# A fused token mixer and MLP on one core: a fixed order of all work, decay tables by exp, the state's sum off TensorE, w2 loaded in thirds, one-tile groups

## The chip, the cores and the metric

One core of a Trainium2 chip. The metric is device time in microseconds (us), median of several executions; lower is better. The kernel before takes 175.2 us. TensorE (PE in the profile) does matmuls and transposes, PEld loads its weights; VectorE is DVE, ScalarE is ACT, GpSimd is POOL, SyncE is SP, which issues most loads.

## The reference

A linear-attention recurrence per head, then a layer norm, an MLP and a residual. Float32 in and out, 4 batches, 8 heads of 48, 768 tokens, model width 384, MLP width 1536:

```python
for t in range(S):
    cur = np.einsum('bhd,bhe->bhde', u[None] * kt, vt)
    y[:, :, t] = np.einsum('bhd,bhde->bhe', rt, state + cur)
    state = w[None, :, :, None] * state + np.einsum('bhd,bhe->bhde', kt, vt)
...
xn = (x - mu) / np.sqrt(var + 1e-06) * g_ln
ch = np.maximum(xn @ w_ch1, 0.0) @ w_ch2
return x + ch
```

Both kernels cut the tokens into 24 tiles of 128. Within a tile the recurrence becomes matrix products: K is scaled by w to a falling power of the token's place, R by w to a rising one, both are transposed, their product is masked to the past, and the rest goes through a running state Z (bf16).

## The kernel before

It is tuned already: the tiles run in a rotation in which the MLP of earlier tiles fills TensorE while attention of the next tile waits for other engines. Four places matter here. The decay tables are made by doubling along the token axis on VectorE, transposed in float32 on TensorE and evicted:

```python
T = const.tile([P, 2 * CK, L + 1], FP32, name="T")
... # T[..., n+1:2n+1] = T[..., 1:n+1] * T[..., n], seven times, on VectorE
for a in (0, 1):
    for kc in range(CK):
        nc.tensor.transpose(out=fps[:, a, kc * P : (kc + 1) * P], in_=src, identity=ident_f[:])
```

The old state is added in PSUM by a matmul with the identity, and VectorE multiplies the sum by the decay of a tile:

```python
nc.tensor.matmul(out=s_ps[:, : HP * E2], lhsT=ident[:], rhs=Z_t[i - 1]..., start=False, ...)
... # + K^T V of this tile
nc.vector.tensor_tensor(out=Z[:], in0=s_ps..., in1=WLZ[:], op=ALU.mult)
```

The MLP works on pairs of tiles (GT = 2), so an up-projection matmul has 256 columns:

```python
hp = ps_h.tile([P, 2, GW], FP32, name="hp")      # GW = 256
for f in range(2):
    for kc in range(CK):
        nc.tensor.matmul(out=hp[:, f, :], lhsT=w1_sb[:, n, kc, fb*P:(fb+1)*P], rhs=xT_t[g][:, kc, :], ...)
nc.scalar.activation(out=hT_t[g][:, 2*m : 2*m+2, :], in_=hp[:], func=ACT.Relu)
```

w1 is loaded in thirds by SyncE between the tiles' loads, scaled by the norm's gain and cast to bf16 by three engines. w2 comes in one load, issued by GpSimd in the second turn of the main loop:

```python
if s == W2_SLOT:                                  # s == 1
    nc.gpsimd.dma_start(out=w2_sb[:], in_=w2_src)
```

Of the kernel before, what the change touches and what calls it, by code (L numbers as in the profile page):

```python
# [8 lines left out]
FP32 = mybir.dt.float32  # L9
# [3 lines left out]
ENG = mybir.EngineType  # L13


@with_exitstack
def kernel(
# [24 lines left out]
    GT = 2  # L42
    GW = GT * P
    E2 = 2 * D
    assert D <= DP and H % 2 == 0 and S % L == 0 and C % P == 0 and F % P == 0
    assert tuple(out.shape) == (B, S, C)

    const = ctx.enter_context(tc.tile_pool(name="const", bufs=1))
    ld = ctx.enter_context(tc.tile_pool(name="ld", bufs=7))
    sb2 = ctx.enter_context(tc.tile_pool(name="sb2", bufs=2))  # L50
    sb3 = ctx.enter_context(tc.tile_pool(name="sb3", bufs=3))
    sm = ctx.enter_context(tc.tile_pool(name="sm", bufs=4))
    xp = ctx.enter_context(tc.tile_pool(name="xp", bufs=14))
    ps_h = ctx.enter_context(tc.tile_pool(name="ps_h", bufs=2, space=bass.MemoryType.PSUM))
    ps = ctx.enter_context(tc.tile_pool(name="ps", bufs=1, space=bass.MemoryType.PSUM))

    ctx.enter_context(
        tc.manual_schedule(
            engines={ENG.PE, ENG.DVE, ENG.Activation, ENG.Pool, ENG.SP}
        )  # L60
    )


    rk_t, vf_t, v_t = {}, {}, {}

    def load(i, k_eng=None):
        b, c = divmod(i, NCH)
        s0 = c * L
        rk = ld.tile([P, 2, H, D], FP32, name="rk")
        vf = ld.tile([P, H, D], FP32, name="vf")  # L70
        (k_eng or nc.sync).dma_start(out=rk[:, 1], in_=k[b, :, s0 : s0 + L, :].rearrange("h t d -> t h d"))
        nc.sync.dma_start(out=rk[:, 0], in_=r[b, :, s0 : s0 + L, :].rearrange("h t d -> t h d"))
        nc.sync.dma_start(out=vf[:], in_=v[b, :, s0 : s0 + L, :].rearrange("h t d -> t h d"))
        rk_t[i], vf_t[i] = rk, vf

    w_c = const.tile([P, CK], FP32, name="w_c")
    nc.sync.dma_start(out=w_c[:], in_=bass.AP(tensor=w.tensor, offset=w.offset, ap=[[1, P], [P, CK]]))
    load(0, nc.scalar)
    w_p = const.tile([P, HP], FP32, name="w_p")
    u_p = const.tile([P, HP], FP32, name="u_p")  # L80
    nc.vector.memset(w_p[:], 0.0)
    nc.vector.memset(u_p[:], 0.0)
    for src, dst in ((w, w_p), (u, u_p)):
        for par in range(2):
            nc.scalar.dma_start(
                out=dst[par * DP : par * DP + D, :],
                in_=bass.AP(tensor=src.tensor, offset=src.offset + par * D, ap=[[1, D], [E2, HP]]),
            )
    g_sb = const.tile([P, CK], FP32, name="g_sb")
    nc.scalar.dma_start(out=g_sb[:], in_=moe_g_ln.rearrange("(kc p) -> p kc", p=P))  # L90
    load(1)
    NW = 3
    FW = F // NW
    w1_f = const.tile([P, NW, CK, FW], FP32, name="w1_f")
    w1_src = moe_w_ch1.rearrange("(kc p) (n f) -> p n kc f", p=P, n=NW)
    for n in range(NW):
        nc.sync.dma_start(out=w1_f[:, n], in_=w1_src[:, n])
    w1_sb = const.tile([P, NW, CK, FW], BF16, name="w1_sb")
    w2_sb = const.tile([P, FK, C], BF16, name="w2_sb")
    w2_src = moe_w_ch2.rearrange("(fk p) c -> p fk c", p=P)  # L100
    load(2)
    load(3)


    ident_f = const.tile([P, P], FP32, name="ident_f")
    make_identity(nc, ident_f[:])
    mask = const.tile([P, P], BF16, name="mask")
    nc.gpsimd.memset(mask[:], 0.0)
    nc.gpsimd.affine_select(
        out=mask[:],  # L110
        in_=mask[:],
        compare_op=ALU.is_ge,
        fill=1.0,
        base=0,
        pattern=[[-1, P]],
        channel_multiplier=1,
    )
    ident = const.tile([P, P], BF16, name="ident")
    nc.vector.tensor_copy(ident[:], ident_f[:])
    expo = const.tile([P, GT], FP32, name="expo")  # L120
    nc.vector.memset(expo[:], -0.5)
    NSC = 3
    sc_bufs = []
    for i in range(NSC):
        t_ = const.tile([P, 2, H, DP], BF16, name=f"sc{i}")
        nc.vector.memset(t_[:, :, :, D:DP], 0.0)
        sc_bufs.append(t_)
    WLZ = const.tile([P, HP, E2], FP32, name="WLZ")
    nc.vector.memset(WLZ[:], 0.0)
    uwI = const.tile([P, HP, 2], BF16, name="uwI")  # L130
    nc.vector.memset(uwI[:], 0.0)


    T = const.tile([P, 2 * CK, L + 1], FP32, name="T")
    nc.vector.memset(T[:, :, 0:1], 1.0)
    nc.vector.tensor_copy(T[:, 0:CK, 1], w_c[:])
    nc.vector.reciprocal(out=T[:, CK : 2 * CK, 1], in_=w_c[:])
    n = 1
    while n < L:
        nc.vector.tensor_tensor(  # L140
            out=T[:, :, n + 1 : 2 * n + 1],
            in0=T[:, :, 1 : n + 1],
            in1=T[:, :, n : n + 1].to_broadcast([P, 2 * CK, n]),
            op=ALU.mult,
        )
        n *= 2
    fps = ps.tile([P, 2, 512], FP32, name="at")
    F2 = const.tile([P, 2, H, D], FP32, name="F2")
    for a in (0, 1):
        for kc in range(CK):  # L150
            src = T[:, CK + kc, 1 : L + 1] if a else T[:, kc, 0:L]
            nc.tensor.transpose(out=fps[:, a, kc * P : (kc + 1) * P], in_=src, identity=ident_f[:])
    nc.scalar.copy(out=F2[:, 0], in_=fps[:, 0, :C].rearrange("p (h d) -> p h d", h=H))
    nc.vector.tensor_copy(out=F2[:, 1], in_=fps[:, 1, :C].rearrange("p (h d) -> p h d", h=H))


    wl = const.tile([P, HP], FP32, name="wl")
    nc.gpsimd.tensor_tensor(out=wl[:], in0=w_p[:], in1=w_p[:], op=ALU.mult)
    n = 2
    while n < L:  # L160
        nc.gpsimd.tensor_tensor(out=wl[:], in0=wl[:], in1=wl[:], op=ALU.mult)
        n *= 2
    assert n == L
    for par in range(2):
        p0 = par * DP
        nc.gpsimd.tensor_tensor(
            out=uwI[p0 : p0 + D, :, par], in0=u_p[p0 : p0 + D, :], in1=w_p[p0 : p0 + D, :], op=ALU.mult
        )
    for par in range(2):
        p0 = par * DP  # L170
        nc.gpsimd.tensor_copy(
            out=WLZ[p0 : p0 + D, :, par * D : (par + 1) * D],
            in_=wl[p0 : p0 + D, :].unsqueeze(2).to_broadcast([D, HP, D]),
        )


    g_neg = const.tile([P, CK], FP32, name="g_neg")

    def scale_w1(n):
        if n == 0:  # L180
            nc.vector.tensor_scalar(
                out=g_neg[:], in0=g_sb[:], scalar1=-1.0, scalar2=None, op0=ALU.mult
            )
        nc.scalar.activation(
            out=w1_sb[:, n, 0], in_=w1_f[:, n, 0], func=ACT.Copy, scale=g_neg[:, 0:1]
        )
        nc.vector.tensor_scalar(
            out=w1_sb[:, n, 1], in0=w1_f[:, n, 1], scalar1=g_neg[:, 1:2], scalar2=None, op0=ALU.mult
        )
        nc.gpsimd.tensor_scalar(  # L190
            out=w1_sb[:, n, 2],
            in0=w1_f[:, n, 2],
            scalar1=g_neg[:, 2:3],
            scalar2=1.0,
            op0=ALU.mult,
            op1=ALU.mult,
        )


    tr_t, cc_t, Z_t, A_t, x_t, mv_t, xn_t, q_t, st = {}, {}, {}, {}, {}, {}, {}, {}, {}  # L200

    def scale(i):
        sc = sc_bufs[i % NSC]
        nc.vector.tensor_tensor(out=sc[:, 1, :, :D], in0=rk_t[i][:, 1], in1=F2[:, 1], op=ALU.mult)  # L204
        nc.gpsimd.tensor_tensor(out=sc[:, 0, :, :D], in0=rk_t[i][:, 0], in1=F2[:, 0], op=ALU.mult)  # L205
        vv = ld.tile([P, H, D], BF16, name="vv")
        nc.gpsimd.tensor_copy(out=vv[:], in_=vf_t[i][:])  # L207
        v_t[i] = vv

    def transposes(i):  # L210
        sc = sc_bufs[i % NSC].rearrange("p a (q e) d -> p (a q) (e d)", e=2)
        tp = ps.tile([P, 2 * HP, P], BF16, name="tr")
        for j in range(2 * HP):
            nc.tensor.transpose(out=tp[:, j, :], in_=sc[:, j, :], identity=ident[:])  # L214
        tr = sb3.tile([P, 2, HP, P], BF16, name="trs")
        nc.scalar.copy(out=tr[:], in_=tp[:].rearrange("p (a q) t -> p a q t", a=2))  # L216
        q = sb2.tile([P, HP, P], BF16, name="q")
        nc.vector.tensor_tensor(out=q[:], in0=tr[:, 0], in1=tr[:, 1], op=ALU.mult)  # L218
        tr_t[i] = tr
        q_t[i] = q  # L220

    def scores(i):
        b, c = divmod(i, NCH)
        tr, q = tr_t[i], q_t[i]
        at = ps.tile([P, 2, HP, P], FP32, name="at")
        for p in range(HP):
            for par in range(2):
                p0 = par * DP
                nc.tensor.matmul(  # L229
                    out=at[:, par, p, :],  # L230
                    lhsT=tr[p0 : p0 + D, 1, p, :],
                    rhs=tr[p0 : p0 + D, 0, p, :],
                    start=True,
                    stop=True,
                )
# [272 lines left out]
```

## Time and profile before

| | before |
|---|---|
| median of 3 | 175.21 us (175.11 to 175.75) |
| span of the profiled execution | 173.4 us |
| TensorE saturated from | 31.0 us |
| last matmul ends | 169.9 us |
| TensorE busy | 85% of the span |

The body by itself, from the end of the ramp to the last matmul (view: busy time by stretch; columns: stretch, its length, busy us of PE, PEld, DVE, ACT, POOL with instruction counts, granted clock, DMA share, GB/s):

```profile
31.00:169.90 138.90, 134.65 (x1523) 101.02 (x1520) 94.72 (x189) 84.39 (x157) 56.09 (x81) 1.00 0.55 115
```

Of 138.9 us TensorE is busy in 134.65; no other engine is busy in more than 95. So a change that only speeds another engine gains nothing here. There are three places to win: the 31 us before it, TensorE's own work, and its last per cents of idle.

### The profile page before, as it was taken

Reading aid. Unit: us, or ns where it says so; the run is one execution under the profiler, and the core shown is the slowest. Engines: PE = TensorE matmul, PEld = TensorE weight load, DVE = VectorE, ACT = ScalarE, POOL = GpSimd, SP = SyncE. Lnnn points to the kernel's source line nnn. Section 1 sums busy time; section 2 is a strip of 40 time slices with the busy share of each in tenths; the row PEclk is TensorE's granted clock in tenths of the full one; section 3 lists DMA queues with packets and bytes.
Section 4 is the critical chain, followed back from the end, with each engine's and each line's share of the span. In section 5 each row is a group of like instructions: output and inputs, shape, how many; then the busy total and the mean of one; then the engine's idle time right before and its main releaser. Section 6 shows DMA issues by size and latency. Waiting matters only on the chain.

```text
span 173.4 us, 4126 instructions
## 1 busy us (share of the span) xinstructions
PE 146.9 (85%) x1646; PEld 110.4 (64%) x1646; DVE 113.9 (66%) x236; ACT 94.6 (55%) x173; POOL 74.7 (43%) x119
## 2 busy tenths in 40 slices
PE   0327453998999999999999999999999999999981
PEld 0215242695786877777768767777778687686640
DVE  4407959549788688678767976786768667840111
ACT  0313273385585774675666647656666577565410
POOL 2292699057426553374255335642752453120000
PEclk9999999999999999999999999999999999999999
DMA  5999999999954755874686568546954011101121
GB/s 98 163 351 316 186 181 177 200 190 150 199 114 95 169 114 104 167 155 89 140 165 147 110 110 183 131 105 135 181 112 119 0 49 45 33 18 45 45 93 46
DMA packets 82739, 22.69 MB, mean 131 GB/s; under 512 B 76960, under 2 KB 81568, under 8 KB 82720
## 3 DMA queue, kind: packets, MB, share of 16 engines
q1 hardware_dynamic: 78896, 21.04, 59.1%
q0 software_dynamic: 1552, 1.18, 4.6%
q10 hardware_dynamic: 2272, 0.20, 1.1%
q8 instruction: 13, 0.21, 0.6%
q14 instruction: 6, 0.05, 0.1%
HBM read 18.88 MB, written 4.72 MB: 136 GB/s over the span
## 4 chain that ended last, share of the span: by engine, by line
PE 76%; DVE 10%; ACT 8%; issue 2%; DMA 1%; POOL 1%; DVEq 0%; ACTq 0%
PE hp L374 27%; PE o L396 25%; PE tr L214 7%; PE at L229 4%; ACT xT L359 3%; ACT trs L216 3%; PE tr L358 3%; PE s L240 2%; PE s L260 2%; PE y L312 2%; DMA w_c<-in_w_dram 1%; PE s L251 1%; PE y L300 1%; DVE ot L405 1%; DVE stats L326 1%
## 5 line engine op out<-in xcount | busy, mean ns | idle before, releaser
L374 PE MATMUL hp<-xT,w_sb 128*128 128x256 bf16 x432 | 58.0, 276 | 2.7 <-ACT xT L359 2.7
L396 PE MATMUL o<-w_sb,hT 128*128 128x384 bf16 x288 | 56.3, 326 | 0.9 <-DVE ot L405 0.8
L381 ACT ACTIVATE hT<-hp 128x512 bf16<-128x512 f32 x72 | 42.9, 598 | 22.6 <-PE hp L374 22.1
L279 POOL TENSOR_TENSOR Vb<-vf,cc 128x384 f32<-128x384 f32 x24 | 20.2, 841 | 66.2 <-ACT cc L277 66.2
L374 PEld LDWEIGHTS <-w_sb 128*128 128x128 bf16 x432 | 40.3, 99 | 9.0 <-issue 3.8
L396 PEld LDWEIGHTS <-hT 128*128 128x128 bf16 x288 | 27.6, 98 | 13.6 <-issue 1.4
L270 DVE TENSOR_TENSOR A<-at,mask 128x512 bf16<-128x512 f32 x48 | 30.7, 682 | 1.3 <-PE at L229 1.3
L216 ACT COPY trs<-tr 128x1024 bf16<-128x1024 bf16 x24 | 24.2, 1009 | 13.2 <-PE tr L214 13.2
L218 DVE TENSOR_TENSOR q<-trs 128x512 bf16<-128x512 bf16 x24 | 12.3, 512 | 25.2 <-ACT trs L216 25.1
L205 POOL TENSOR_TENSOR sc<-rk,F 128x384 bf16<-128x384 f32 x24 | 23.9, 997 | 2.4 <-DMA rk<-in_r_dram 2.4
L405 DVE SCALAR_TENSOR_TENSOR ot<-o,rs,x 128x384 f32<-128x384 f32 x24 | 14.6, 609 | 14.6 <-PE o L396 14.6
L214 PE MATMUL tr<-ident,sc 128*128 128x128 bf16 x192 | 16.7, 234 | 7.4 <-POOL sc L205 5.7
L214 PEld LDWEIGHTS <-sc 128*128 128x128 bf16 x192 | 13.6, 105 | 10.2 <-POOL sc L205 6.5
L322 DVE TENSOR_TENSOR x<-y,Vb 128x384 f32<-128x384 f32 x24 | 13.4, 556 | 9.1 <-PE y L312 9.0
L337 ACT ACTIVATE xn<-x,mv 128x384 bf16<-128x384 f32 x24 | 14.8, 617 | 0.7 <-DVE mv L330 0.7
L277 ACT COPY cc<-s 128x8 f32<-128x8 f32 x24 | 4.0, 166 | 20.2 <-PE s L260 17.8
L359 ACT COPY xT<-tr 128x384 bf16<-128x384 bf16 x24 | 11.5, 480 | 5.5 <-PE tr L358 5.5
L204 DVE TENSOR_TENSOR sc<-rk,F 128x384 bf16<-128x384 f32 x24 | 14.4, 599 | 0.0
L207 POOL CAST vv<-vf 128x384 bf16<-128x384 f32 x24 | 14.3, 595 | 0.0
L326 DVE BATCH_NORM_STATS2 stats<-x 128x6 f32<-128x384 f32 x24 | 13.5, 561 | 0.8
L358 PE MATMUL tr<-ident,xn 128*128 128x128 bf16 x72 | 8.2, 225 | 4.3 <-ACT trs L216 4.3
L229 PE MATMUL at<-trs 48*128 48x128 bf16 x192 | 10.4, 233 | 1.7 <-ACT trs L216 1.7
(49 smaller groups left out, 119.1 us busy)
## 6 DMA issues: line engine op xcount, KB each, us to landing
rk<-in_r_dram SPq DMA_DIRECT2D x24, 192.0 KB, 4.1
vf<-in_v_dram SPq DMA_DIRECT2D x24, 192.0 KB, 4.2
out_dram<-ot SPq DMA_DIRECT2D x24, 192.0 KB, 2.0
rk<-in_k_dram SPq DMA_DIRECT2D x23, 192.0 KB, 3.4
w_f<-in_moe_w_ch_dram SPq DMA_DIRECT2D x3, 768.0 KB, 6.1
w_sb<-in_moe_w_ch_dram POOLq DMA_DIRECT2D x1, 1152.0 KB, 12.5
rk<-in_k_dram ACTq DMA_DIRECT2D x1, 192.0 KB, 3.6
w_p<-in_w_dram ACTq DMA_DIRECT2D x2, 0.8 KB, 4.3
```

What stands on the lines that cost most here:

```text
L205: nc.gpsimd.tensor_tensor(out=sc[:, 0, :, :D], in0=rk_t[i][:, 0], in1=F2[:, 0], op=ALU.mult)
L214: nc.tensor.transpose(out=tp[:, j, :], in_=sc[:, j, :], identity=ident[:])
L216: nc.scalar.copy(out=tr[:], in_=tp[:].rearrange("p (a q) t -> p a q t", a=2))
L229: nc.tensor.matmul(out=at[:, par, p, :], lhsT=tr[p0 : p0 + D, 1, p, :], rhs=tr[p0 : p0 + D, 0, p, :], start=True, stop=True,)
L270: nc.vector.tensor_tensor(out=A[:, par], in0=at[:, par], in1=mask[:].unsqueeze(1).to_broadcast([P, HP, P]), op=ALU.mult,)
L279: nc.gpsimd.tensor_tensor(out=Vb[:], in0=vf_t[i][:], in1=cc[:].unsqueeze(2).to_broadcast([P, H, D]), op=ALU.mult)
L326: nc.vector.bn_stats(out=stats[:], in_=x[:])
L359: nc.scalar.copy(out=xT_t[g][:, :, j * P : (j + 1) * P], in_=tp[:, :CK, :])
L374: nc.tensor.matmul(out=hp[:, f, :], lhsT=w1_sb[:, n, kc, fb * P : (fb + 1) * P], rhs=xT_t[g][:, kc, :], start=(kc == 0), stop=(kc == CK - 1),)
L381: nc.scalar.activation(out=hT_t[g][:, 2 * m : 2 * m + 2, :], in_=hp[:], func=ACT.Relu)
L396: nc.tensor.matmul(out=o[:, :C], lhsT=hT_t[g][:, fk, j * P : (j + 1) * P], rhs=w2_sb[:, fk, :], start=(fk == 0), stop=(fk == FK - 1),)
L405: nc.vector.scalar_tensor_tensor(out=ot[:], in0=o[:, :C], scalar=rs_t[g][:, j : j + 1], in1=x_t[i][:], op0=ALU.mult, op1=ALU.add,)
```

## The change

Its intent is to have the machine's whole order, for every engine and every load, written down in one list that a search made, and to take work from TensorE and from the long start. The main loop is gone. A string of steps, each "name, index, engine", is walked once, and the instructions come out in this order:

```diff
-    scale(0)
-    transposes(0)
-    for s in range(NT):
-        ...                       # rotation of scale, scores, center, load, fill, transposes, values
+PLAN = """
+LK,0,- MI,0,g MW,0,v TL,0,s MP,0,v WU,36,- IW2,0,g WB,0,- LR,0,- MM,0,g LN,0,s IW2,2,g
+FK,0,s FR,0,s IW2,1,g SR,0,v ROWS,0,- LK,1,- SK,0,v UGP,0,- LR,1,- TR,0,- SK,1,v UGC,0,v
+...                               # 24 tiles: LK LR LV loads, SK SR scaling, TR transposes, AT scores,
+"""                               # UP RL up-projection and Relu, DN down-projection, STO store
```

Read for the start: the first tile's K (LK,0) is loaded, 36 dummy matmuls are to warm TensorE's clock (WU), and the three w2 loads (IW2) stand before nearly everything else. The parts:

```diff
+    def FK_(i, e):                # decay tables in token rows: exp(ln w * place)
+        nc.scalar.activation(out=Fk[:], in_=ln_b[:], func=ACT.Exp, scale=pow_i[:, 1:2])
+    def UGP(i, e):                # w, u, g from rows to columns: 11 fp32 matmuls with a 1x1 one
+        ... nc.tensor.matmul(out=t[:, ...], lhsT=flat[:, q, :], rhs=one[:], start=True, stop=True)
-                nc.tensor.matmul(out=s_ps[:, : HP * E2], lhsT=ident[:], rhs=Z_t[i - 1]...)
+    def ZU(i, e):                 # old state added on VectorE ...
+            nc.vector.tensor_tensor(out=ZS(i)[:], in0=s3, in1=ZZ(i - 1)[:], op=ALU.add)
+    def ZD(i, e):                 # ... and decayed on GpSimd
+        times("g", ZZ(i)[:], ZS(i)[:], WLZ[:])
-    w2_src = moe_w_ch2.rearrange("(fk p) c -> p fk c", p=P)
+    w2_src = moe_w_ch2.rearrange("(n p fk) c -> p n fk c", p=P, n=NW)
+        o, s = w1_sb[n][kc][:], w1_f[n][:, kc].rearrange("p (q a) -> p a q", a=FB)
-    GT = 2
+GROUPS = [1, 1, 1, ...]           # 24 groups of one tile: up matmuls of 128 columns
-        for par in range(2):
-            nc.vector.tensor_tensor(out=A[:, par], in0=at[:, par], in1=mask...)
+        mask_part(i, 0, 2)        # the mask in one instruction of 1024 columns
```

The new w2 layout gives each partition one long run per third; the order of w1's columns has to follow it, which is why the scaling now reads its input with a step of four elements. The 11 matmuls of UGP are 22 in the profile, which shows two for each; the text counts the 22 and calls them the row matmuls. Thirteen of 72 Relu evictions, most of R's scaling (17 of 24) and some copies move to VectorE.

## The prediction

> **What bounds the kernel now.** I read four views of the profile in this order: the head of the page, the busy time by stretch, the engine timeline of two steady tiles, and the start of the chain that ended last.
>
> The page says that TensorE is busy 85% of the span, and where it is not:
>
> ```profile
> span 173.4 us, 4126 instructions
> PE 146.9 (85%) x1646; PEld 110.4 (64%) x1646; DVE 113.9 (66%) x236; ACT 94.6 (55%) x173; POOL 74.7 (43%) x119
> PE   0327453998999999999999999999999999999981
> DMA  5999999999954755874686568546954011101121
> ```
>
> One digit is a slice of 4.3 us. The first seven slices are the ramp: TensorE mostly idle, the DMA engines full. From the eighth to the end it is full. By stretch (columns: length, then busy us of PE, PEld, DVE, ACT, POOL, clock, DMA share, GB/s):
>
> ```profile
> 0.00:31.00 31.00, 12.28 (x126) 9.35 (x127) 18.61 (x47) 10.23 (x16) 18.64 (x38) 1.00 1.18 210
> 62.00:74.00 12.00, 11.80 (x144) 9.02 (x143) 9.10 (x20) 7.52 (x14) 5.55 (x8) 1.00 0.65 132
> 170.00:173.40 3.40, 0.00 (x0) 0.00 (x0) 0.47 (x1) 0.00 (x0) 0.00 (x0) 1.00 0.16 58
> ```
>
> So there are a ramp of 31 us, a body of 139 us bound by TensorE, and a tail of 3.4 us (last matmul, its eviction, its store). Busy time overlaps itself on TensorE, so I take the real cost of a matmul from the distance between starts of successive groups (timeline; start, length, engine, line, count):
>
> ```profile
> 62.18 1.47 PE L374 MATMUL hp<-xT,w_sb 128*128 128x256 bf16 x12
> 63.49 0.61 PE L214 MATMUL tr<-ident,sc 128*128 128x128 bf16 x8
> 63.93 1.46 PE L396 MATMUL o<-w_sb,hT 128*128 128x384 bf16 x8
> 65.24 0.33 PE L358 MATMUL tr<-ident,xn 128*128 128x128 bf16 x3
> 66.13 0.81 PE L374 MATMUL hp<-xT,w_sb 128*128 128x256 bf16 x6 [0.20 <-ACT xT L359]
> ```
>
> Twelve up-projection matmuls of 256 columns take 63.49-62.18 = 1.31 us, 109 ns each; eight down-projection matmuls of 384 columns take 1.31 us, 164 ns each; eight transposes of 128 columns, each with its own weights, take 0.44 us, 55 ns each. In the same way a tile of attention costs 0.44 (chunk transposes), 0.33 (scores), 0.12 (bonus), 0.16 (old state added through the identity), 0.17 (new state), 0.17 (transposes of the normalised row), 0.17 and 0.20 (values): 1.76 us. A tile's MLP costs 18x0.109 + 12x0.164 = 3.93 us. One tile is 5.69 us, two are 11.4, and the period read from the timeline is 11.9 (scores start at 61.40 and again two tiles later at 73.30): about 4% real idle in the body.
>
> The ramp, from the chain of waits in order of time:
>
> ```profile
> 10.39 1.00 POOL sc L205
> 18.42 1.11 issue
> 25.65 2.10 DVE w_sb L187 x2
> 28.92 1.02 ACT trs L216
> 31.10 2.65 PE hp L374 x12
> ```
>
> The first transpose waits for a decay table (log-doubling on VectorE, six fp32 transposes, two evictions, then GpSimd); the first up-projection waits for the second tile of a pair, which queued behind weight scaling. And it runs cold: 12 matmuls in 2.65 us against 1.31 later.
>
> **What the Trainium skill says.** (1) "TensorE: Matmul & The Clock Gate", section "Back-to-back issue gap", gives N/2.4 + 2.5 ns for an isolated matmul, but about 81 ns per matmul at N=128 for a stream where each has its own weight load. That matters, since the change cuts the up-projection to N=128. The trace disagrees with 81: eight such pairs took 55 ns each, which is the isolated formula (55.8). I use 55. (2) "SBUF — State Buffer", section "Who interferes with whom": a VectorE instruction with both inputs in SBUF and a GpSimd instruction that reads SBUF shut each other out. The trace agrees: the scaling of K on VectorE has a median of 548 ns, but one took 1325 ns, started 0.08 us after a GpSimd multiply of 0.99 us. (3) "DMA: Bandwidth & Descriptors", section "Issuing engines are not separate DMA queues" with "Queues, rings and completion order": all issuers share the same 16 engines. So moving the w2 load to time zero does not add bandwidth; it takes it from the first tiles. The ramp shows the 16 engines full whoever issues.
>
> **The change, part by part.**
>
> TensorE work. The up-projection goes from 432x109 ns = 47.1 us to 864x55.5 = 48.0 us: +0.9. The identity matmul for the state goes: 16x0.16 = -2.6. The rest is the same. Total ideal work before: 24x5.69 = 136.6, less the state matmuls (about 0.33 us) that the first and the last chunk of each of the four batches do without: 134. After: 132.3, plus a dozen one-column fp32 matmuls in the ramp. Only 1.7 us less: the change does not live from less TensorE work.
>
> The ramp is where it can win, and it is DMA-bound. From the trace: a 192 KB load of q, k or v in 192-byte packets moves at 185 to 188 GB/s, so 1.05 us; w1 at about 400 GB/s, so 1.95 us per third. w2 before was 1552 packets; the new split gives each partition one contiguous run per third. I estimate 2.36 MB read at w1's 400 GB/s: 5.9 us. Before full speed the plan needs, in issue order, eleven chunk loads (tiles 0 to 3 but one), three thirds of w1 and all of w2: 11x1.05 + 3x1.95 + 5.9 + 0.6 (small rows) = 23.9 us, from 2 us on: 26 us. Add the scaling of the last third (0.7 to 1.0) and the up-projection that it frees: TensorE is saturated from about 27.5 us, not from 31. More telling: it has by then done more. Before, at 31 us, no MLP was done, and 5 us of attention. After, the first third of w1 and one-tile groups let the up-projection begin at about 21 us; by 27.5 I count five up blocks of 0.67 us (3.3) and three tiles' attention (5.0): 8.3 us. And 36 warm-up matmuls cannot hold the clock for 20 us, but the early blocks will have warmed it, which saves the 1.3 us of cold running.
>
> The decay tables by Ln and Exp (three ScalarE instructions of about 0.5 us on a broadcast row) bring the first chunk transposes from 11.4 us to about 7. This is hidden: the loads end the ramp.
>
> Sum. Before: 31 us + 134 - 5 = 129 us of ideal work left + 1.3 cold + 8.5 idle = 169.8, where the last matmul ends. The idle is the 4% of the body (5.5), the rest at its two ends, where the pair of tiles makes the down-projections of the last tiles wait for one output buffer. After: 27.5 + (132.3 - 8.3 = 124) + 7 of idle (the body's 4%, and 1.5 at the ends) + tail 3.4 = 161.9 us of span. The time before exceeds its span by 175.2 - 173.4 = 1.8; so 163.7 us, 6 to 7% less.
>
> VectorE is where it can lose. From the rows of the page: x, statistics, aggregate and output are 13.4 + 13.5 + 4.4 + 14.6 = 45.9 us, unchanged. The mask in one instruction of 1024 rather than two at 1.28 us a pair: an estimated 1.2, so 28.8. The product for the bonus, 22 at 0.51: 11.3. Scaling of K and of R, 19 + 17 at 0.6: 21.6 (R was on GpSimd). State sum 20 at 0.55: 10.9. New on VectorE: 13 of the 72 Relu evictions at an estimated 0.68 (the mask of 512 from PSUM): 8.8; and 12 coefficient copies, 9 value casts, 7 centrings, 6 transposed-row copies: 2 + 3.6 + 2.8 + 2.9. Setup 3. Sum 142 us, 86% of 164 us, up from 66%. ScalarE falls from 94.6 to about 85. GpSimd rises to about 90: the state decay 16x1.0, and the inverse root twice as often (24x0.92 = 22 instead of 11), against 17 R scalings less.
>
> **The rivals.** (a) VectorE becomes the bound. For: 142 us and 58 two-SBUF instructions that GpSimd, half busy, can hold up; at 0.2 us each that is 12 us more, and VectorE would fill 94%. In-order queues at 86 to 94% on one side and 96% on the other couple tightly, so TensorE would wait for masks and Relu. Against: 142 is still below TensorE's 132.3 plus the ramp's wait, and attention runs ahead of the MLP. It would give 168 to 174. (b) The searched order fits the machine better than the old rotation: idle falls to 1%, and w1 lands earlier. For: the old idle has a few regular causes (0.20 us at the row copy). That gives 159 to 161. (c) The skill's 81 ns holds in long runs of N=128: 864x(81-55) = +22 us and a time near 186. Against: the eight transposes, and values matmuls with 128-column weights that follow each other at 25 ns. (d) w2 at the front starves the first tiles so that the ramp ends at 31 again: 167 to 168, since the up blocks done early still count.
>
> **Range and chances.** The sum says 163.7; I go to 164.5, since (a) costs more than (b) gives. With no idle the count gives 157, which I don't believe; the mild form of (a) is 170: 8 in 10 between 159.5 and 170.5. Faster by over 2% means below 171.7: 0.88. Within 2%: 0.09. Slower: 0.03, which needs (c) or (a) at its worst.
>
> **What would show it.** First chunk transpose near 7 us; first up-projection near 21; TensorE full from 27 to 28; its last matmul near 159, and a tail of 3.4. Groups of 128-column up matmuls must follow at 55 ns. VectorE's busy share near 86%, and in the idle list of TensorE a growing share ended by VectorE. I am wrong if the up matmuls space at 70 ns or more, if TensorE idles over 8% in the body, or if the ramp's loads do not end near 26 us.

## The result, and the profile after

| | before | after |
|---|---|---|
| median | 175.28 us | 169.62 us (168.95 to 169.93, 4 runs) |
| ratio of the fast runs | 1 | 0.9666 (95% interval 0.9642 to 0.9691) |
| span of the profiled execution | 173.4 us | 167.4 us |
| TensorE saturated from | 31.0 us | 33.5 us |
| from there to the last matmul's end | 138.9 us | 130.4 us |
| tail | 3.5 us | 3.5 us |

A ratio is the mean time of one kernel's fast runs over the mean of the other's fast runs of the same rounds, so it isn't quite the ratio of the medians quoted. Executions over 1.5% slower than the fastest of the same kernel are left out of the means. The change is faster by 3.3%, and inside the predicted range. But the forecast was about 6%, and the table says where the rest stayed: the body gave 8.5 us, and the ramp, which was to give 3.5, took 2.5. The sum, -8.5 + 2.5 = -6.0, is the difference of the spans.

The page of the kernel after:

```profile
span 167.4 us, 5077 instructions
PE 151.7 (91%) x2114; PEld 123.2 (74%) x2114; DVE 128.4 (77%) x265; ACT 81.9 (49%) x142; POOL 91.0 (54%) x142
PE   7397358998999999999999999989999999999991
DMA  4999979800598899999997979890111110101121
```

TensorE shows work in the first slices, but those are the warm-up and small matmuls; the row is full from the seventh or eighth slice on, as before. By stretch:

```profile
0.00:33.50 33.50, 23.52 (x236) 21.09 (x236) 19.20 (x50) 14.28 (x21) 18.32 (x38) 1.00 0.92 207
33.50:163.90 130.40, 128.14 (x1882) 102.10 (x1879) 108.61 (x214) 67.60 (x122) 72.67 (x105) 1.00 0.54 121
```

In the body TensorE is busy 128.14 of 130.40 us, and VectorE 108.6. The end of the ramp is where the fifth up-projection block ("up block": twelve matmuls, one tile by one third of w1) has passed TensorE. The engine timeline of TensorE in the ramp, and two lines of a steady tile for the spacing (start, length, engine, line, operation, sizes, count, and in brackets the idle before it with its releaser):

```profile
12.31 0.61 PE L343 MATMUL tr<-ident,scr 128*128 128x128 bf16 x4
...
25.59 1.44 PE L494 MATMUL hp<-xT,w_sb 128*128 128x128 bf16 x12
27.92 1.44 PE L494 MATMUL hp<-xT,w_sb 128*128 128x128 bf16 x12 [0.57 <-ACT xT L198]
29.58 1.45 PE L494 MATMUL hp<-xT,w_sb 128*128 128x128 bf16 x12
31.69 0.83 PE L494 MATMUL hp<-xT,w_sb 128*128 128x128 bf16 x12
32.84 0.84 PE L494 MATMUL hp<-xT,w_sb 128*128 128x128 bf16 x12 [0.32 <-ACT w_sb L311]
...
65.80 1.50 PE L494 MATMUL hp<-xT,w_sb 128*128 128x128 bf16 x24
67.14 0.24 PE L393 MATMUL s<-uwI,q 128*128 128x2 bf16 x4
```

First chunk transposes at 12.31 us (forecast 7), first up block at 25.59 (21), and the first three blocks take 1.44 us instead of 0.83. The fifth waits for a piece of w1 that ScalarE scaled. In the steady tile 24 up matmuls take 67.14 - 65.80 = 1.34 us, 55.8 ns each, as forecast.

Why so late? The chain of waits of the kernel after:

```profile
3.59 9.75 DMA kf<-in_k_dram
13.36 0.56 DVE sck L203
...
17.00 0.34 POOL WLZ L298
...
22.46 1.05 PE tr L343 x8
```

The K load of the second tile is issued at 3.59 us and lands 9.75 us later; VectorE, which works in order, sits at its scaling and so do the small copies behind it, the decay of a tile on GpSimd (which ends at 17.7), and what hangs on them. And SyncE, which issues the loads (its timeline; the second number is how long the issue took):

```profile
3.59 0.40 SPq L321 DMA_DIRECT2D kf<-in_k_dram  x1
...
5.93 7.18 SPq L327 DMA_DIRECT2D vf<-in_v_dram  x2
...
23.65 0.63 SPq L304 DMA_DIRECT2D w_f<-in_moe_w_ch_dram  x1
```

Two V loads take 7.18 us to issue, all that stands behind them in the list is pushed back, and the last third of w1 is issued only at 23.65. The w2 loads explain it if the queues say so. From 8 to 14 us, the DMA view gives for GpSimd's queue (q0, w2 alone) and SyncE's (q1) the packets, MB and share of the 16 engines' time:

```profile
q0 software_dynamic: 249, 0.66, 55.6%
q1 hardware_dynamic: 3123, 0.59, 51.7%
```

Half of the engines' time goes to weights that the first down-projection needs well after the first up-projection.

### The profile page after: what moved, and what is told of

It reads as the page before. It is cut to its first block, busy times and chain, and to the rows that moved or that the text cites. A ratio compares the mean times of both kernels' runs of the same rounds, so it can differ in the third digit from the quotient of the medians.

```text
span 167.4 us, 5077 instructions
## 1 busy us (share of the span) xinstructions
PE 151.7 (91%) x2114; PEld 123.2 (74%) x2114; DVE 128.4 (77%) x265; ACT 81.9 (49%) x142; POOL 91.0 (54%) x142
## 4 chain that ended last, share of the span: by engine, by line
PE 55%; DVE 16%; DMA 11%; SPq 6%; issue 4%; ACT 4%; POOL 3%; DVEq 0%; POOLq 0%
PE hp L494 21%; PE o L522 19%; DMA kf<-in_k_dram 9%; PE tr L343 4%; PE at L362 3%; DVE sck L203 3%; PE tr L479 3%; DVE A L372 3%; SPq L324 2%; DMA rf<-in_r_dram 2%; PE y L443 2%; DVE ot L532 2%; ACT trs L198 2%; DVE stats L453 2%; DVE scr L203 2%
## 5 line engine op out<-in xcount | busy, mean ns | idle before, releaser
L494 PE MATMUL hp<-xT,w_sb 128*128 128x128 bf16 x864 | 58.7, 223 | 1.3 <-ACT xT L198 0.6
L494 PEld LDWEIGHTS <-w_sb 128*128 128x128 bf16 x864 | 52.2, 100 | 4.2 <-issue 1.3
L198 ACT COPY trs<-tr 128x1024 bf16<-128x1024 bf16 (+1 forms) x25 | 23.4, 944 | 21.2 <-PE tr L343 21.2
L372 DVE TENSOR_TENSOR A<-at,mask 128x1024 bf16<-128x1024 f32 (+1 forms) x26 | 29.3, 1131 | 1.1 <-PE at L362 0.7
L203 POOL TENSOR_TENSOR Z<-ZS,WLZ 128x384 bf16<-128x384 f32 x16 | 17.0, 1066 | 5.8 <-DVE ZS L419 5.4
L203 DVE TENSOR_TENSOR sck<-kf,Fk 128x384 bf16<-128x384 f32 x19 | 13.0, 690 | 7.4 <-DMA kf<-in_k_dram 6.7
L474 POOL TENSOR_TENSOR rs<-rs,expo 128x1 f32<-128x1 f32 x24 | 13.6, 569 | 2.0
L203 DVE TENSOR_TENSOR scr<-rf,Fr 128x384 bf16<-128x384 f32 x17 | 10.5, 621 | 5.2 <-ACT Fr L264 4.9
L471 POOL TENSOR_SCALAR rs<-mv 128x1 f32<-128x1 f32 x24 | 6.2, 258 | 13.7 <-DVE mv L457 12.5
L512 DVE TENSOR_SCALAR hT<-hp 128x512 bf16<-128x512 f32 x13 | 8.8, 681 | 2.3 <-PE hp L494 2.2
L343 PE MATMUL tr<-ident,scr 128*128 128x128 bf16 x96 | 10.0, 230 | 0.7 <-DVE scr L203 0.7
```

The source lines that it names most:

```text
L198: nc.scalar.copy(out=out, in_=in_)
L203: engines[e].tensor_tensor(out=out, in0=in0, in1=in1, op=ALU.mult)
L343: nc.tensor.transpose(out=t[:, a * HP + q, :], in_=flat[:, q, :], identity=ident[:])
L372: nc.vector.tensor_tensor(out=AA(i)[:, a:b].rearrange("p e q t -> p (e q) t"), in0=psum["at", i][:, a:b].rearrange("p e q t -> p (e q) t") ...
L474: nc.gpsimd.tensor_tensor(out=rs[g][:], in0=rs[g][:], in1=expo[:, :n], op=ALU.pow)
L494: nc.tensor.matmul(out=t[:, a * gw : (a + 1) * gw], lhsT=w1_sb[n][kc][:, fb], rhs=xT(g)[:, kc, :gw], start=(kc == 0), stop=(kc == CK - 1),)
```

## The experiments

Two theories of the long ramp were open, and both act in it at the same time. The first: w2 at the front takes the DMA engines from the first tiles and from w1. The rival, the second: the way in which w, u and g get to their columns (three row loads, the 22 row matmuls, three copies) is the path, since those matmuls stand ahead of the first transposes from 7.56 to 12.31 us. Two further questions were what the identity matmul is worth, and whether the step of four in the scaling or the cold clock costs time. Twelve kernels ran. All edits are against the kernel after.

**w2_late.** The three w2 loads after the decay of a tile on GpSimd:

```diff
-... WU,36,- IW2,0,g WB,0,- ... LN,0,s IW2,2,g FK,0,s FR,0,s IW2,1,g SR,0,v ... WL,0,g ...
+... WU,36,- WB,0,- ... LN,0,s FK,0,s FR,0,s SR,0,v ... WL,0,g IW2,0,g IW2,2,g IW2,1,g ...
```

> The three loads of w2 move behind the decay-power chain on GpSimd (from 1.5-4 us to about 17 us); nothing else changes. Theory 1 (w2 in front takes the DMA engines from the first chunks): the second K chunk lands near 7.5 us instead of 13.3, the first up-projection starts near 22 us instead of 25.6, and the time falls by 3 to 4 us to about 166. Theory 2 (the 22 tiny fp32 matmuls for w, u and g hold the first chunk transposes until 12.3 us): the transposes stay at 12.3 us and the time moves by less than 1 us. Theory 3 (the loss is in the body, VectorE): no change.

Measured: 166.78 us, ratio 0.9507 (0.9437 to 0.9577; three fast runs, the fourth, 167.66 us, counts as slow), against 0.9666 for the change. The w2 loads go out at 14.94 us. The second tile's K now lands 3.4 us after its issue at 3.59, at 7.0; the two V loads take 1.28 us to issue; the first up block starts at 23.53 and the last third of w1 is issued at 16.75 instead of 23.65. The ramp ends at 31.6, with the fifth block, here the second half of one line:

```profile
30.24 1.50 PE L489 MATMUL hp<-xT,w_sb 128*128 128x128 bf16 x24
```

The first theory stands; the move alone is worth some 2.8 us (0.0159 of 175).

**params_dma and both.** w, u and g by small column loads on ScalarE's queue, as in the kernel before, without the 22 matmuls; `both` has the w2 move too.

```diff
 def ROWS(i, e):
-    nc.sync.dma_start(out=w_row[:, :, :D], in_=w.rearrange("(o h) d -> o h d", o=1))   # and u, g
+    nc.scalar.dma_start(out=w_p[...], in_=<column of w>)                              # and u, g
-UGP,0,-
```

> w, u and g come by small column loads as in the kernel before, and the 22 fp32 matmuls go; w2 stays in front. Theory 2: the first chunk transposes start near 7.6 us instead of 12.3 and the time falls by 3 to 4 us. Theory 1: the transposes start earlier, but the second K chunk still lands near 13 us and everything behind it on VectorE with it, so less than 1 us is gained.

> w2 late and the parameters by small loads together. If the two causes only hide each other, this gains clearly more than the sum of the two alone: about 4 to 6 us, a time of 164 to 165.5 us, which is what was predicted. If theory 1 alone holds: the same as w2 late alone. Theory 3: no change.

Both gave a wrong result: the loads stood in the list ahead of the memsets of the same tiles, so the memsets waited for them and wiped them out. Their times (171.13 us, 0.9769, and 166.41 us, 0.9498) are told for completeness, and no verdict rests on them: a wait of VectorE for small loads that the list alone caused is a delay of its own.

**state_pe.** The identity matmul for the state again, and no GpSimd decay.

```diff
-ZPE = []
+ZPE = [1, 2, 3, 4, 7, 8, 9, 10, 13, 14, 15, 16, 19, 20, 21, 22]
-ZD,...        # all 16
```

> The state sum goes back to TensorE: 16 identity matmuls of 384 columns come back, 16 GpSimd multiplies go, VectorE's state instruction stays one of the same size. If TensorE bounds the body: 16 x 0.16 = 2.6 us longer, about 172. If GpSimd and VectorE waits make the idle of the body (theory 3): no longer than after, 169.6, or shorter.

Measured: 170.63 us, 0.9758 (0.9705 to 0.9811), so 0.9758 - 0.9666 = 0.9% or 1.6 us slower than the change; the intervals stand 0.0014 apart. From 38 to 158 us, by stretch, with the matmuls back and then without:

```profile
38.00:158.00 120.00, 118.94 (x1764) 95.42 (x1762) 104.19 (x206) 63.45 (x113) 57.52 (x87) 1.00 0.57 128
```

```profile
38.00:158.00 120.00, 117.96 (x1752) 94.34 (x1751) 103.80 (x206) 63.23 (x113) 70.03 (x100) 1.00 0.58 128
```

TensorE gets 16 x 0.16 = 2.6 us more over the whole kernel, and most of it shows in the time. That speaks for TensorE as the bound of the body. GpSimd loses 12.5 us of work, and that isn't without use: TensorE's idle in this stretch falls from 2.04 to 1.06 us. The longest wait of TensorE in the body of the kernel after, for V as GpSimd casts it, is gone:

```profile
113.14 0.33 PE L406 MATMUL s<-vv,sck 128*128 128x96 bf16 x4 [0.76 <-POOL vv L200]
```

So taking the state's sum off TensorE saved 2.6 us there and, as these two traces read, gave about 1 us back in waits.

**params_dma2 and both2.** The same two, with the memsets ahead of the loads.

```diff
-LK,0,- MI,0,g MW,0,v TL,0,s ... ROWS,0,- ... UGP,0,- ...
+LK,0,- MI,0,g MW,0,v ROWS,0,- TL,0,s ...
```

> The earlier parameter run again, mended (its loads stood before the memsets of the same tiles, which waited for them and overwrote them). w, u, g by small column loads, no tiny fp32 matmuls, w2 still in front. Theory 1: the first transposes move from 12.3 to about 8 us, the second K chunk still lands near 13 us, gain under 1 us (169 us). Theory 2: gain of 3 us or more.

> w2 late and the mended parameter loads. With w2 late alone the chain of waits ran through the parameter matmuls (6.2 to 11.1 us) and the decay powers behind them. If the two causes hide each other, this gains another 2 to 3 us over w2 late alone: first up-projection near 20 us, time about 164. If not: 166.5 as with w2 late alone.

Measured: params_dma2 168.49 us, 0.9624 (0.9589 to 0.9660); both2 168.65 us, 0.9619 (0.9567 to 0.9671); both correct. params_dma2 does what it was meant to: the first transposes come at 8.84 us instead of 12.31. But the first up block starts at 25.20 instead of 25.59, and the time moves by 0.4% with overlapping intervals. The second theory falls as long as w2 stands in front: the row matmuls were hidden behind the loads.

both2 was a surprise: with both edits it is no better than params_dma2, and its ratio lies above that of w2_late, with intervals that just overlap. GpSimd no longer waits for the row matmuls, so "after the decay of a tile" comes earlier, and w2 goes out at 11.61 us. Then the R load of the fourth tile is the one to suffer (chain of waits of both2):

```profile
12.10 13.16 DMA rf<-in_r_dram
```

The last third of w1 is issued at 22.48 again. Its ramp ends at 32.1 us, half a microsecond after that of w2_late; the other 1.4 us between their spans lie in the body, and I have no cause for them.

**both2_plain.** both2 with w1 and w2 in their natural column order, so that the scaling reads without a step.

```diff
-w1_f[n][:, kc].rearrange("p (q a) -> p a q", a=FB)
+w1_f[n][:, kc].rearrange("p (a q) -> p a q", a=FB)
-w2_src = moe_w_ch2.rearrange("(n p fk) c -> p n fk c", p=P, n=NW)
+w2_src = moe_w_ch2.rearrange("(n fk p) c -> p n fk c", p=P, n=NW)
```

> The same, and w1 is read contiguously by the scaling again (w2 split by rows of 128 as before). Scaling of one 128x512 piece took 1.2 us on ScalarE and 1.4 on GpSimd against 0.72 and 0.79 in the kernel before. Expect these to fall back to 0.7-0.8 us and the start of the last first-round up block to come 0.5 to 1 us earlier: 0.5 us off the time. w2's packets become four times as many and a quarter as large, which is now hidden.

Measured: 168.67 us, 0.9609 (0.9549 to 0.9670). By source line, ScalarE's pieces (minimum, median and maximum ns, then first and last start), in the kernel after and here (in the kernel before, where there was no step either, the median was 721 ns):

```profile
L311 ACT ACTIVATE w_sb<-w_f,g_neg x4: 1200/1222/1227, 20.0 to 31.6; 128x512 bf16<-128x512 f32 x4
```

```profile
L291 ACT ACTIVATE w_sb<-w_f,g_neg x4: 707/718/724, 14.4 to 29.4; 128x512 bf16<-128x512 f32 x4
```

The step of four costs 0.5 us a piece and nothing that shows in the time: nine pieces, spread over three engines, lie beside waits for loads.

**no_warm.** Without the 36 dummy matmuls (`-WU,36,-`).

> The change as it is, without the 36 warm-up matmuls. If they are too early to help, since TensorE idles or runs slowly from 5 to 25 us: no change (169.6, within 0.5%). If they do keep the clock up: 1 us longer or more.

Measured: 169.84 us, 0.9685 (0.9619 to 0.9751) against 0.9666: no difference to be seen where w2 stands at the front. The first two up blocks take 1.44 us with or without the dummies, which end at 5.0 us, twenty before the first block.

**w2_last.** The w2 loads after the scaling of a piece of w1 (`SW,6,g`), behind all that the ramp needs.

```diff
-... IW2,0,g ... IW2,2,g ... IW2,1,g ... SW,6,g SR,3,v ...
+... SW,6,g IW2,0,g IW2,2,g IW2,1,g SR,3,v ...
```

> The change with one edit: w2 is issued after the last scaling piece of the second w1 third on GpSimd (about 22 us), behind all of w1 and the first four tiles. With w2 at 11.6 us (w2 late and small parameter loads together) the fourth R chunk took 13 us to land and the last third of w1 landed at 28.7 us: w2 had only taken the engines from other loads. Theory 1: now the fourth R chunk and the last third land before 22 us, the fifth up block starts near 28 us, and the time is 165 to 166, at or below w2 late alone (0.951). If w2's place does not matter beyond the first chunks: equal to w2 late alone.

Measured: 166.16 us over 6 runs of which two were slow; the fast ones give 0.9481 (0.9439 to 0.9523). This is the lowest ratio, below the change's 0.9666 with intervals well apart, and correct; it beats both kernels. ("Slow" is told by the time alone on one core; with all six its mean is 166.46 us, still 3 below the change. What the two slow runs have in common is told below the table.) From 8 to 14 us w2 is gone from the DMA view, and the other queue moves 1.65 MB instead of 0.59:

```profile
q1 hardware_dynamic: 3720, 1.65, 104.7%
```

SyncE issues the last third at 16.68:

```profile
16.68 0.99 SPq L299 DMA_DIRECT2D w_f<-in_moe_w_ch_dram  x1
```

It lands 6.4 us later, at 23.1 instead of 23.65 + 6.0 = 29.65: earlier by 6.55, about the 5.96 us of the 16 engines' time that w2 takes. TensorE's timeline:

```profile
20.64 1.44 PE L489 MATMUL hp<-xT,w_sb 128*128 128x128 bf16 x12
...
29.00 0.79 PE L489 MATMUL hp<-xT,w_sb 128*128 128x128 bf16 x11 [0.94 <-DVE w_sb L308]
```

The first up block starts at 20.64, where the prediction had it (21). The fifth ends at 29.6: 3.9 us earlier, not 6.5. What holds it is in the timelines of VectorE and of GpSimd:

```profile
25.67 3.27 DVE L308 TENSOR_SCALAR w_sb<-w_f,g_neg 128x512 bf16<-128x512 f32 x1
```

```profile
25.48 0.84 POOL L420 TENSOR_TENSOR Vb<-vf,cc 128x384 f32<-128x384 f32 x1
26.30 1.20 POOL L310 TENSOR_SCALAR w_sb<-w_f,g_neg 128x512 bf16<-128x512 f32 x1
27.49 0.98 POOL L198 TENSOR_TENSOR Z<-ZS,WLZ 128x384 bf16<-128x384 f32 x1
```

One scaling piece, 0.84 us on VectorE in the kernel after, takes 3.27 here, and ends 0.47 us after the third GpSimd instruction in a row (28.94 against 28.47). It reads as VectorE shut out by GpSimd. both3 and both3_loads show the same, 3.37 and 3.23 us beside the same three; in the kernel after these three stand in a row too, but there GpSimd's scaling is the long one, 1.60 us instead of 1.20. No run took just this away, so it's read, not shown.

By stretch, the body is what it was:

```profile
29.70:159.60 129.90, 128.00 (x1880) 102.05 (x1878) 109.09 (x215) 67.07 (x120) 72.32 (x104) 1.00 0.57 127
```

129.9 us against 130.4: the change of w2's place is a change of the ramp alone.

**both3, both3_loads, both3_loads_warm.** w2_last with the small column loads; then also the loads of tiles 4 to 9 ahead of the first store, since the DMA engines idle from about 33 to 42 us in the kernel after (share 0.03), while SyncE's queue waits to store the first output; then also dummy matmuls in TensorE's gaps, to keep its clock warm.

```diff
+LK,0,- MI,0,g MW,0,v TL,0,s ROWS,0,- ...                  # both3: w2_last, and no UGP
+... LV,3,- LK,4,- LR,4,- LV,4,- ... LV,9,- ... STO,0,-     # both3_loads
+WU,56,- ... WU,16,- AT,0,- ... WU,12,- Y,1,- ...           # both3_loads_warm (five such groups)
```

> The same w2 place, and w, u, g by small column loads after the table load. Theory 2 (parameter matmuls bind once w2 is out of the way): another 1.5 to 2.5 us over w2 last, 163 to 164. If the two do not add: equal to w2 last.

> The same, and the loads of tiles 4 to 9 go on the load queue before the first store instead of behind it (the DMA engines stood still from about 32 to 41 us and were full from 50 to 100 us; TensorE waited for an R chunk near 108 us). Expect the idle of 0.8 us near 110 us and the small gaps from 38 to 62 us to shrink: 0.5 to 1.5 us. If these loads in turn delay w2: no gain or a loss.

> The same, with dummy matmuls in TensorE's waits from 5 to 24 us (36 become 56, and five groups of 8 to 16), so that the clock is up when the first up blocks come. In every run so far three or four up blocks of 12 took 1.44 us instead of 0.83. If the cold clock costs time: first blocks at 0.83 us and 1 to 2 us less. If the last third of w1 sets the end of the ramp: under 0.5 us.

Measured: both3 166.12 us, 0.9523 (0.9479 to 0.9566, one slow run of six left out); both3_loads 165.57 us, 0.9491 (0.9457 to 0.9526, six fast runs); both3_loads_warm 166.56 us, 0.9542 (0.9505 to 0.9578, two slow runs left out). So the parameters bring nothing that shows here either, beside the fast runs of w2_last. But in the profiled executions both3's edit did not do what it was meant to: its first transposes come at 9.58 us, those of w2_last at 8.69. So whether the row matmuls bind once w2 is out of the way is not settled. The earlier loads fill the DMA engines (share 1.00 from 30 to 42 us, against 0.46 in both3) and may be worth 0.3%, 0.6 us, but the intervals overlap: inconclusive. The wait of 0.76 us that they were to shrink is still there, at 109.65 us; it is the one for GpSimd's cast. The dummy matmuls do what they were meant to, the up blocks take 0.83 us from the first one on, and the time doesn't fall: the fifth block waits for w1 all the same, till 28.98. The one profile of this kernel is of a slow run, so nothing more is read from it. Of the versions that beat both kernels, w2_last and both3_loads can't be told apart by their fast runs; both3_loads had no slow one (its six span 1.7 us, those of w2_last 4.4).

All profiled executions with a correct result side by side, but for both3_loads_warm, whose one is slow (the ramp's end is the start of the fifth up block's last group plus 56 ns for each of its matmuls; where the view merges two blocks, the group's end less 0.17 us, the time by which a last matmul outlasts the start of a next):

| kernel | w2 issued | last third of w1 issued | ramp ends | span | span less ramp |
|---|---|---|---|---|---|
| after | 1.5 | 23.65 | 33.5 | 167.4 | 133.9 |
| state_pe | 1.5 | 23.85 | 34.2 | 168.2 | 134.0 |
| no_warm | 1.5 | 22.60 | 33.2 | 167.0 | 133.8 |
| params_dma2 | 1.5 | 22.23 | 33.2 | 167.4 | 134.2 |
| both2 | 11.6 | 22.48 | 32.1 | 166.8 | 134.7 |
| both2_plain | 11.9 | 18.69 | 31.6 | 166.6 | 135.0 |
| w2_late | 14.9 | 16.75 | 31.6 | 164.9 | 133.3 |
| both3 | 24.5 | 17.18 | 30.5 | 165.9 | 135.4 |
| both3_loads | 24.5 | 17.37 | 30.5 | 163.6 | 133.1 |
| w2_last | 23.6 | 16.68 | 29.6 | 163.1 | 133.5 |

Read the columns for w2 and for the ramp's end: 33.2 to 34.2 with w2 at the front, about 32 with it in the middle, about 30 with it behind w1. The last column does not follow any edit; it scatters from 133.1 to 135.4, and that limits what these runs can resolve.

One pattern stands in the scatter. The mean granted clock of an execution is either within 0.4% of full or between 0.92 and 0.95 (both3_loads_warm apart). Where it is lower, the page's clock row shows a stretch at half speed in the ramp; here that of w2_last:

```profile
PEclk9955558999999999999999999999999999999999
```

The kernel after was profiled in an execution whose row reads full throughout, and its first up blocks took the same 1.44 us. The difference lies ahead of them. TensorE's timeline of w2_last, then of the kernel after, where the first eight row matmuls run:

```profile
6.18 1.02 PE L266 MATMUL s<-one,w_row 1*128 1x1 f32 x8 [1.18 <-DMA w_row<-in_w_dram]
```

```profile
7.56 1.83 PE L271 MATMUL s<-one,w_row 1*128 1x1 f32 x8 [2.56 <-DVE scr L203]
```

So I read a lowered mean as the mark of an execution in which the dummy matmuls did warm the clock, which then fell back to half, and a full one as not having risen before the up blocks. Its one rise, at about 31 us in the kernel after, where the blocks go from 1.44 to 0.83, leaves no mark in the row. All four executions of no_warm have it full. In w2_late the two lowered ones took 165.15 and 166.28 us, the two full ones 167.29 and 167.66; in both2_plain 166.68 against 168.6 to 168.8. But the change itself, params_dma2 and both3_loads show no such order. What the warm-up is worth, and when, stays open.

This bears on w2_last. Its two slow runs (167.32 and 168.98 us) are its two full ones, so its 0.9481 stands on lowered executions alone, while three of the change's four are full. The two full ones of w2_last alone are at 168.15 / 174.65 = 0.963 of the kernel before, hardly below the 0.966 of the change's three: for such executions these runs don't show a gain in time from w2_last. What holds at equal marks is this. Profiled full, the ramp ends at 33.5 in the change and at 31.6 in w2_late. Profiled lowered, it ends at 33.2 in params_dma2 and at 29.6 in w2_last, and all four lowered times of w2_last (164.61 to 166.50) lie below all four of params_dma2 (167.84 to 169.55). And without row matmuls w2 last gains in full executions too: 165.35 and 165.39 us in both3_loads against 168.58 in params_dma2.

## Why the prediction was right or wrong

By the sum it forecast 163.7 us (then moved to 164.5); the profiled run took 169.8. That this lies in the range is partly luck: the upper end, 170, was drawn for a mild form of rival (a), VectorE as the bound, and what brought the time near it was the ramp. Of the three signs of being wrong that the prediction named, the third came true: the ramp's loads ended not near 26 us but at 29.65. Term by term ("ideal" counts each matmul at its full-speed spacing, without waits):

| term | forecast | measured | difference |
|---|---|---|---|
| TensorE saturated from | 27.5 | 33.5 | +6.0 |
| ideal work left then | 124 | 124.1 | +0.1 |
| body beyond it | 7 | 130.4 - 124.1 = 6.3 | -0.7 |
| tail | 3.4 | 3.5 | +0.1 |
| time over the span | 1.8 | 169.79 - 167.4 = 2.4 | +0.6 |

**The step that failed is the ramp**: "it is DMA-bound ... 23.9 us, from 2 us on: 26 us", then "TensorE is saturated from about 27.5 us, not from 31". Its +6.0 has parts that the trace gives. The loads: the last third of w1 landed at 29.65 instead of 26, +3.65. Up to then the 16 engines had spent 27.6 us of their time (the DMA share times the length, added over the stretches up to 29.65) against the 23.9 counted; the volume that I counted was right, w2 took 5.96 us for my 5.9, but the tile loads issued behind the third shared the engines with it (two of them would be 2.1 at my 1.05 each), and the rest isn't accounted for. Then the plan: ScalarE began its scaling only at 31.56, +1.91, since in the fixed order it stands behind the Relu of the third up block, which was late and cold. The scaling took 1.22 instead of about 0.85, +0.37, and a gap of 0.06. Together 5.99.

The error behind the terms is that I counted w2 as volume. The sum was to say when *all* had landed, and I let the ramp end there, wherever w2 stood. But the fifth up block doesn't need w2. Placed in front it delays the loads behind it, and with them the scaling and the first up blocks; placed last it delays none that the ramp needs. The prediction had the premise in hand: that w2 at time zero "takes it from the first tiles". Rival (d) drew the conclusion, but with an end of ramp at 31 and a time of 167 to 168, it too was 2.5 us short, and it carried little weight in the 164.5. w2_last shows the reverse: w2 out of the way, the first up block comes at 20.64, and the w1 that I had at 26 lands at 23.1.

**Saturated with 8.3 us of work done: right** (8.2, counted from the matmul groups in the ramp), only 6 us later. So the body's gain of 8.5 us, by my count of ideal work, is 3.2 more work done in the ramp (8.2 against 5.0), 1.7 less work, the 1.3 of cold running, which now falls before the ramp's end, and 2.3 less time beyond the ideal (from 138.9 - 129 - 1.3 = 8.6 to 6.3). The last two are arithmetic; what of the 2.3 is the searched order's merit was not tested alone.

**Early blocks warm the clock: wrong.** Three up blocks took 1.44 us each, with gaps between them. (That the 36 dummy matmuls can't hold the clock was right: in the row of w2_last it is at half speed from the third slice, 8.2 us, on.) As far as the one profile with the clock kept warm tells, a slow one, it cost little: the fifth block waited for w1 all the same.

**First transposes at 7: wrong**, 12.31, because the 22 row matmuls, which I had not placed, ran ahead of them for 4.75 us. "This is hidden: the loads end the ramp" was right: taking them away moved the transposes to 8.84 and not the time.

**Less TensorE work, 1.7 us: right in kind.** Putting the identity matmuls back cost 1.6 us of the 2.6 they occupy; the rest fits the waits that GpSimd's decay costs.

**128 columns at 55 ns: right**, 55.8; rival (c) falls. **VectorE 142 us: the sum holds, the share doesn't.** The means of VectorE's groups times their counts give about 144 (the mask 1.21 us for my 1.2, the Relu 0.68 for 0.68), but consecutive instructions overlap, and the busy time of the page is 128.4 us, 77% and not 86%. In the body it is 108.6 of 130.4 us while TensorE has 128.1, so rival (a), VectorE as the bound, falls; of the waits of TensorE that the timeline lists from 38 to 158 us, 0.70 of 1.67 us end with VectorE. Rival (b), an order that fits better, is true in the body and by less than it said: time beyond the ideal fell from 8.6 of 138.9 us to 6.3 of 130.4, not to 1%, and the order wasn't tested by itself.

**Not foreseen:** the scaling with a step of four (1.22 for 0.72 us on ScalarE); harmless. Nor was TensorE's wait of 0.76 us for GpSimd's cast, between 109 and 114 us in every profile of a correct run but that of state_pe, which has no decay on GpSimd. The open end: why no variant gets below 0.948.

## What to carry to other kernels

When loads bound a start, don't add up their volumes: for the event that ends the start, list what it needs, in issue order, and count only what is ahead of it or shares the engines with it. A large load that is needed late cost the last third of w1 about its transfer time here when it went first (6.55 us for 5.96), and no load of the ramp when it went last. A fixed order makes such a move an edit of three tokens, but each in-order engine will then also pass a delay on to all that stands behind it.

## What the Trainium skill lacked or had wrong

- "TensorE: Matmul & The Clock Gate", section "Back-to-back issue gap", gives about 81 ns per matmul at 128 columns for a stream with a weight load each. Here 24 such matmuls with 24 weight loads took 1.34 us, 55.8 ns each; the page's formula for the isolated case fits, and the 81 doesn't hold for this kernel. The same page, section "What's actually happening", says that the clock rises after about 3.4 us of sustained work, in a window that runs freely. The 36 dummy matmuls kept TensorE busy for 4.02 us and yet the clock seems to have risen in some executions only (eight row matmuls in 1.02 or in 1.83 us); an estimate from the page's 3.4 us is that 4.02 us covers a whole window only for a part of its phases. And a record without any change didn't mean a warm clock here: the clock row of the kernel after reads full while its blocks take 1.44 us instead of 0.83.
- "DMA: Bandwidth & Descriptors", section "Queues, rings and completion order", says that each DMA engine takes turns between queues packet by packet. It lacks what this means for a load in small packets beside one with long runs: w2 took 55.6% of the engines' time from 8 to 14 us, and the K load issued at 3.59 us, in packets of 192 bytes, took 9.75 us to land, against 3.3 without w2 in front. It also has no figure for how long an issue holds SyncE while earlier loads are in flight: 7.18 us for two loads here, 1.32 us for the same two in w2_last.
- "GPSIMD Engine Reference", section "Performance pitfalls for Q7 kernels", puts reads of SBUF with a step of over 8 bytes at about 50% more per element. GpSimd's scaling with a step of 16 bytes took 1.34 us against 0.77 without, 74% more. (The page speaks of kernels written for this engine; here it is a built-in multiply.) I found no figure for a step of 16 bytes on the pages of the other two engines, where it cost as much: 1.22 against 0.72 us on ScalarE, 0.84 against 0.485 on VectorE.
